# First sequence's 50-point transform with x as the stationary operand

## The chip, the cores and the metric

The kernel runs on one core of a Trainium2 chip. A core has a matrix engine (TensorE, PE in the profile; its weight loads are shown as PEld), a vector engine (DVE), a scalar engine (ACT), GpSimd (POOL) and a sync engine (SP), each with its own queue of instructions, and 16 DMA engines that serve all queues. Matmuls multiply a stationary operand, loaded first, with a moving one; their results go to PSUM, from where DVE or ACT fetch them. The metric is the device time of one execution in microseconds (us); lower is better.

## The reference

The input x has 8 sequences of 3200 positions with 256 channels. Each sequence is filtered in the frequency domain, and the result goes through a gated convolution:

```python
X = np.fft.rfft(x, axis=1)
Yr = Xr @ w_r - Xi @ w_i + b_r
Yi = Xr @ w_i + Xi @ w_r + b_i
Yr, Yi = soft threshold of each by 0.01
y = np.fft.irfft(Yr + 1j * Yi, n=3200, axis=1)
gate = sigmoid(causal depthwise convolution of y with conv_w, 5 taps)
out = (gate * (y @ w_val)) @ w_out
```

The weights `w_val`, `conv_w` and `w_out` come as float64 and are turned into float32 by integer operations on DVE. Channel matmuls split their operands into a high and a low part (three products each), transforms use plain f32.

## The kernel before

A transform of 3200 points is split as 50 x 64: position n = 64 n2 + n1. For each sequence b there are three stages, named in the code as follows.

- `p1(b, u, at)`, u from 0 to 7: the 50-point transform over n2. The table `f1` is stationary, x moves: positions n1 and 64 - n1 are taken together, in two halves of the partitions (50 rows at partition 0, 50 at partition 64). Each piece loads 4 + 4 positions (line 554, a helper that splits a load into 48 and 2 rows), makes its products into PSUM (lines 594, 599, 601), copies one half (ACT, line 607), adds and subtracts the two ("folds", DVE, line 613) and stores the result in DRAM as `a_dram` (lines 554 and 631). The store is there because the next stage needs another order of rows: the frequency and the position's half on the partitions.
- `p2(b, d, at)`, d from 0 to 6: loads rows of `a_dram` (line 650), makes the 64-point transform (`s2`, line 668, with `a` stationary and the table `f2` moving), splits the result into high and low parts, multiplies by the channel matrices (`mix_sum`, line 786, and `mix`, line 782), applies the threshold (lines 794, 796), transforms back over 64 points (`s1i`, line 737) and stores in DRAM as `z_dram` (line 753).
- `positions`, `conv`, `gated`: load `z_dram` (line 554), transform back over 50 points (`s2i`, line 848), convolve (lines 896, 899), project (lines 882, 878), and write the output (line 960).

Nothing is issued in the order of the Python loops. Every piece is given to a planner (`Plan`) with an engine, a cost, a due time made from the weights in the table `O`, and what it uses and sets. `Plan.order` simulates the engines: an engine takes among the pieces that are ready, within a slack, the one with the earliest due time, and that order is what each engine's queue holds. Buffers are slots of rotating pools (`SLOTS`); a piece that opens a buffer waits until the slot's former users are done. DMAs of nearly all kinds are issued from SP's queue. Where the planner sees PE idle between the times in `FILL`, it puts in matmuls of zeros (line 363), and at the start it puts matmuls of an idle buffer (`warm`, line 987).

For the first sequence `p1` has a form of its own (`early`): its loads are issued at once, the first on two queues, into buffers that later serve other ends (`x`, `zl`, `y_hl`). Four groups of warming lie between its pieces. The loads and casts of the channel matrices wait for some of these pieces (`BEHIND`, `START`), and later constants and the second sequence's loads of x wait for the first sequence's stores (`STORED`).

Of the kernel before, what the change touches and what calls it, by code (L numbers as in the profile page):

```python
# [10 lines left out]
F32 = mybir.dt.float32  # L11
# [21 lines left out]
def dft_constants():  # L33
# [67 lines left out]
    out = {"f1": f1.reshape(NH, N2, P), "f2": f2, "g1": g1, "g2": g2.reshape(Q, 2 * Q)}  # L101
# [169 lines left out]
CLOCK = ((28000, 1.6), (45000, 1.2))  # L271
FILL = 36000, 200000
# [9 lines left out]
def act(n, kind="copy"):  # L282
# [9 lines left out]
O = {'spread': -91.8948,  # L292
     'hold': 1.0724,
     'together': 1.2701,
     'later': -3.6572,
     'load_x': 9.9589,
     'p1': 0.1254,
     'p1_step': 1.2361,
     'load_a': -5.3199,
     's2': -1.7149,  # L300
     's1i': 1.553,
     'p3': 1.0966,
     'load_z': -28.9681,
     'y': 11.7985,
     'conv': 25.53,
     'val': 6.1049,
     'gate': -22.7084,
     'project': 7.8156,
     'late_val': 6.023,
     'late_out': 14.484,  # L310
     'turn': -55.8644,
     'pre': -4.984,
     'mix_sum': -1.4205,
     'p1_1': -7.3343,
     'load_x_1': -7.2435,
     'p1_2': -1.5627,
     'p3_0': 0.9988}
WARM = 2, 1, 1, 1, 8
# [8 lines left out]
def fourier_filter_then_gated_conv(ctx: ExitStack, tc: tile.TileContext, x, w_r, w_i, b_r, b_i,  # L327
                                   w_val, conv_w, w_out, f1, f2, g1, g2, out):
# [27 lines left out]
    y_sb = const.tile([P, 2, (N1 + KC - 1) * N2], F32, name="y_sb")  # L356
    mid_sb = const.tile([P, 2, 2, N2], F32, name="mid_sb")
# [47 lines left out]
    def sums(at):  # L405

        n = 2 * D
        for k, (name, sc, op) in enumerate((("w_n", -1.0, ALU.subtract), ("w_d", 1.0, ALU.subtract))):
            key = ("st", name)

            def make(k=k, key=key, sc=sc, op=op):
                r, i = (tl["st", m][:, 0:n] for m in (("w_r", "w_i") if k == 0 else ("w_i", "w_r")))
                out = room(key, "acc", 2 * D)
                tl[key] = out.rearrange("p (j d) -> p j d", j=2)
                nc.vector.scalar_tensor_tensor(out=out, in0=r, scalar=sc, in1=i, op0=ALU.mult, op1=op)
            add(at + 0.1 * k, "DVE", dve(n), make, [("st", "w_r", 0), ("st", "w_i", 0), *START], [key + (0,)], {key: "acc"})
# [75 lines left out]
    def load_bias(at):  # L492
# [23 lines left out]
        add(at, "PE", 2700, spread, [("b", 0, 0), ("b", 0, 1), ("turn", "p1", 7)], [k2 + (0,)], {k2: "ps_2"}, mode="f")  # L516
# [41 lines left out]
    START = [("turn", "start", h) for h in range(NH)]  # L558
# [5 lines left out]
    def p1(b, u, at):  # L564

        kx, kp, ks, ka = ("x", (b, u)), ("p1", (b, u)), ("s1", (b, u)), ("a_dram", b)
        early = b == 0
        x_tag = ("x" if u < 3 else "zl" if u < 6 else "y_hl") if early else "x"
        s_tag = ("s1", "g_hl", "xs")[u % 3] if early else "s1"
        p_tag = "ps_2"  # L570
        rows = ROWS

        def load(h):
            xt = room(kx, x_tag, 4 * D) if h in (0, None) else tl[kx]
            src = x[b].rearrange("(n m) c -> n (m c)", m=N1)
            for g in range(NH) if h is None else (h,):
                eng = QUEUES[g][1] if early and u < BOTH else nc.sync
                lo = (N1 - 3 - 4 * u if g else 4 * u) * D
                n = 3 * D if g and u == 0 else 4 * D
                by_rows(eng, xt[half(g), 0:n], src[:, lo:lo + n], rows)  # L580
                if n < 4 * D:
                    by_rows(eng, xt[half(g), n:], src[:, NM * D:(NM + 1) * D], rows)
        if early:
            for h in range(NH):
                add(-100 + u, QUEUES[h][0] if u < BOTH else "SP", 650, lambda h=h: load(h), (), [kx + (h,)], None if h else {kx: x_tag}, kb=200)
        else:
            add(at + O["load_x"] + O["load_x_1"] * (b == 1), "SP", 1300, lambda: load(None), STORED if b == 1 else (),
                [kx + (0,), kx + (1,)], {kx: x_tag}, kb=400, chain="x")

        def products():  # L590
            xt, p = tl[kx], two_banks(kp, p_tag)
# [42 lines left out]
        if early:  # L634
            STORED.append(("stored", 0, u))
        add(at + 0.02, "SP", 1500 + 1500 * (u == 0), store, [ks + (0,), ks + (1,)],
            [key] + ([STORED[-1]] if early else []), {ka: "a_dram"} if u == 0 else None, kb=400)


    def p2(b, d, at):  # L640
# [10 lines left out]
        add(at + O["load_a"], "SP", 700, load, A_KEYS[b], [ka + (0,)], {ka: "a"}, kb=128 * nt, chain="a")  # L651
# [3 lines left out]
        def s2(i):  # L655
            if i == 0:
                two_banks(k2, "ps_2")
            if last:
                for c in range(2):
                    nc.tensor.matmul(tl[k2][:, 0, c * P:(c + 1) * P], tl[ka][:, 0, c * P:(c + 1) * P], f2_sb[:, (NT - 1) * N1:], start=True, stop=True)  # L660
                return
            p = tl[k2].rearrange("p h (c t k) -> p h c t k", c=2, t=4)
            for t in (2 * i, 2 * i + 1):
                for c in range(2):
                    for h in range(NH):
                        for e in range(2):
                            rows = slice(h * HP, (h + 1) * HP)
                            nc.tensor.matmul(p[e * HP:(e + 1) * HP, h, c, t, :], tl[ka][rows, t, c * P + e * HP:c * P + (e + 1) * HP],  # L668
# [407 lines left out]
```

## Time and profile before

| | us |
|---|---|
| median of 3 runs (lowest, highest) | 858.8 (857.43, 858.82) |
| the profiled execution | 859.73 |
| its span, first to last instruction | 857.8 |
| PE busy in the span | 821.0 |
| DVE busy in the span | 736.2 |
| ACT busy in the span | 593.7 |

The mean granted TensorE clock is 0.973 of full speed; 162.27 MB were moved by DMA. The page divides the span into 40 slices of 21 us and gives, per slice, the busy tenths of each engine and the clock in tenths. A stretch view gives the same for chosen times. In the views, `L668` is line 668 of the kernel, `SPq` the sync engine's queue as it issues DMAs, `[0.79 <-DMA a<-a_dram]` an idle time of the engine in us and what ended it; `x58` counts instructions. An f32 matmul shows as two records of weight load and matmul.

### The profile page before, as it was taken

The numbers are of one execution on the slowest core, as the hardware profiler recorded it, in microseconds if no ns is written. First come the engines' busy times: TensorE is split into PE (matmuls) and PEld (weight loads), VectorE is DVE, ScalarE is ACT, GpSimd is POOL, SyncE is SP. The second block draws the span as 40 slices with busy tenths as digits, with TensorE's granted clock in tenths as the row PEclk, the third lists the DMA queues.
The fourth block names the chain that finished last, engine by engine and source line by source line (L and its number), as shares of the span: only waits on it lengthen the run. The fifth ranks groups of instructions, "written<-read, shape, count | busy, mean of one in ns | idle before, by whom it ended". The sixth has DMA issues, their size and how long they took to land.

```text
span 857.8 us, 23810 instructions
## 1 busy us (share of the span) xinstructions
PE 821.0 (96%) x9866; PEld 700.7 (82%) x9866; DVE 736.2 (86%) x1006; ACT 593.7 (69%) x903; POOL 4.5 (1%) x12
## 2 busy tenths in 40 slices
PE   8878867999999999999999999999999999999997
PEld 2456656889888988889988989899888999998874
DVE  3345679799998999899989998999989998998795
ACT  2234635778777786778777886878777787776753
POOL 0000000000000000000000000000001000000000
PEclk7888979999999999999999999999999999999999
DMA  6688889867886569776796759876895576225422
GB/s 169 182 190 224 246 214 250 228 179 191 209 234 185 165 180 258 203 204 174 224 245 195 192 175 248 206 206 187 231 234 158 157 200 193 71 83 173 133 76 96
DMA packets 125909, 162.27 MB, mean 189 GB/s; under 512 B 12528, under 2 KB 100234, under 8 KB 125802
## 3 DMA queue, kind: packets, MB, share of 16 engines
q1 hardware_dynamic: 125598, 160.34, 68.1%
q8 instruction: 78, 1.28, 0.7%
q10 hardware_dynamic: 204, 0.41, 0.2%
q14 instruction: 29, 0.24, 0.1%
HBM read 82.06 MB, written 78.64 MB: 187 GB/s over the span
## 4 chain that ended last, share of the span: by engine, by line
PE 69%; DVE 13%; DMA 9%; ACT 4%; SPq 3%; issue 2%; DVEq 0%; ACTq 0%
PE o_ps L882 13%; PE y_ps L782 12%; PE v_ps L882 11%; PE y_p L848 10%; PE y_ps L786 6%; DMA x<-in_x 4%; PE p L594 4%; PE s L668 4%; PE z_ps L737 4%; DVE acc L899 4%; PE v_ps L878 2%; SPq L554 2%; DMA zl<-z_dram 1%; DVE acc L933 1%; DVE gated L390 1%
## 5 line engine op out<-in xcount | busy, mean ns | idle before, releaser
L899 DVE SCALAR_TENSOR_TENSOR acc<-y_sb,cw_sb,acc 128x800 f32<-128x800 f32 x256 | 263.0, 1047 | 16.1 <-ACT acc L896 15.6
L782 PEld LDWEIGHTS y_ps<-w_sb,xs 128*128 128x128 f32 x1152 | 144.3, 191 | 28.4 <-DVE y_ps L788 12.4
L782 PE MATMUL y_ps<-w_sb,xs 128*128 128x256 f32 x1152 | 156.3, 286 | 11.1 <-DVE y_ps L788 11.0
L882 PE MATMUL o_ps<-gated,wo_sb 128*128 128x400 f32 x744 | 150.8, 349 | 0.8 <-DVE gated L390 0.8
L882 PEld LDWEIGHTS o_ps<-gated,wo_sb 128*128 128x128 f32 x744 | 134.6, 188 | 4.1 <-DVE gated L390 1.1
L882 PE MATMUL v_ps<-y_hl,wv_sb 128*128 128x400 f32 x648 | 128.4, 346 | 0.5 <-DVE s L613 0.5
L882 PEld LDWEIGHTS v_ps<-y_hl,wv_sb 128*128 128x128 f32 x648 | 115.4, 188 | 1.1 <-PE y_ps L786 0.7
L613 DVE TENSOR_TENSOR s<-p,s 128x512 f32<-128x512 f32 (+2 forms) x144 | 89.3, 626 | 27.5 <-ACT s L607 16.4
L848 PEld LDWEIGHTS y_p<-g_sb,zl 100*64 100x64 f32 x2048 | 89.1, 137 | 11.7 <-ACT y_ps L764 3.5
L848 PE MATMUL y_p<-g_sb,zl 100*64 100x100 f32 x2048 | 97.4, 251 | 0.7 <-DMA zl<-z_dram 0.5
L786 PE MATMUL y_ps<-w_sb,xs 128*128 128x256 f32 x576 | 90.0, 293 | 7.6 <-ACT y_ps L764 7.6
L786 PEld LDWEIGHTS y_ps<-w_sb,xs 128*128 128x128 f32 x576 | 79.3, 194 | 20.9 <-ACT y_ps L764 9.0
L794 ACT ACTIVATE tp<-y_ps,nlam 128x512 f32<-128x512 f32 (+1 forms) x104 | 70.0, 674 | 25.1 <-PE y_ps L782 25.1
L388 ACT CAST gated<-acc 128x800 fp32r<-128x800 f32 x62 | 53.3, 859 | 30.7 <-DVE acc L933 30.5
L601 PE MATMUL p<-x,f_sb 50*64 50x512 f32 x240 | 72.2, 654 | 1.7 <-DMA x<-in_x 1.7
L933 DVE TENSOR_TENSOR acc<-v_ps,acc 128x800 f32<-128x800 f32 x64 | 62.9, 984 | 11.4 <-PE v_ps L878 5.5
L796 DVE SCALAR_TENSOR_TENSOR tp<-y_ps,tp 128x512 f32<-128x512 f32 (+1 forms) x104 | 68.6, 661 | 4.1 <-ACT tp L794 4.0
L594 PE MATMUL p<-x,f_sb 50*64 50x512 f32 x256 | 71.6, 647 | 0.1
L668 PEld LDWEIGHTS s<-f_sb,a 64*64 64x64 f32 x3072 | 53.7, 137 | 19.5 <-issue 11.6
L909 ACT ACTIVATE acc<-acc 128x800 f32<-128x800 f32 x64 | 55.8, 878 | 16.3 <-DVE acc L899 16.0
L958 ACT COPY o<-o_ps 128x800 f32<-128x800 f32 x63 | 51.8, 822 | 21.3 <-PE o_ps L882 15.8
L716 DVE TENSOR_TENSOR sx<-s,sx 128x512 f32<-128x512 f32 x48 | 33.0, 688 | 38.2 <-ACT xs L713 37.2
(92 smaller groups left out, 1031.3 us busy)
## 6 DMA issues: line engine op xcount, KB each, us to landing
out<-o SPq DMA_DIRECT2D x126, 200.0 KB
a<-a_dram SPq DMA_DIRECT2D x96, 256.0 KB
z_dram<-z_t SPq DMA_DIRECT2D x48, 512.0 KB
zl<-z_dram SPq DMA_DIRECT2D x64, 384.0 KB
a_dram<-s SPq DMA_DIRECT2D x120, 192.0 KB
x<-in_x SPq DMA_DIRECT2D x119, 192.0 KB
a_dram<-s SPq DMA_DIRECT2D x120, 8.0 KB
x<-in_x SPq DMA_DIRECT2D x119, 8.0 KB
```

What stands on the lines that cost most here:

```text
L594: nc.tensor.matmul(p[k * HP:(k + 1) * HP, 0, :], f1_sb[half(0), 0:HP], xt[half(0), k * 512:(k + 1) * 512], start=True, stop=True)
L601: nc.tensor.matmul(dst, f1_sb[half(1), 0:HP], back[:, 2 * k:2 * k + 2, :], start=True, stop=True)
L613: nc.vector.tensor_tensor(out=st()[lo:hi, h, n], in0=tl[kp][lo:hi, 0, n], in1=st()[lo:hi, 1, n], op=(ALU.add, ALU.subtract)[h])
L668: nc.tensor.matmul(p[e * HP:(e + 1) * HP, h, c, t, :], tl[ka][rows, t, c * P + e * HP:c * P + (e + 1) * HP], f2_sb[rows, (4 * d + t) * N1: ...
L782: nc.tensor.matmul(p[:, 1 - r, :], xm(hx, c, r, i), w_sb[:, m, hw, c, :], start=False, stop=k == 5, skip_group_check=True)
L786: nc.tensor.matmul(tl[ky][:, 0], sm(hx, c, i), w_sb[:, 0, hw, c, :], start=False, stop=k == 5, skip_group_check=True)
L794: nc.scalar.activation(out=buffer(kt, "tp", [P, 2, D])[:, 0:n], in_=tl[ky][:, 0:n], func=AF.Relu, bias=nlam)
L796: add(at + 0.2, "DVE", dve(n * D), lambda: nc.vector.scalar_tensor_tensor(out=tl[kt][:, 0:n], in0=tl[ky][:, 0:n], scalar=LAM, in1=tl[kt][: ...
L848: nc.tensor.matmul(dst[e * HP:(e + 1) * HP], zt[0:Q, m, c * P + e * HP:c * P + (e + 1) * HP], g, start=True, stop=True)
L882: nc.tensor.matmul(p[:, e, 0:TB], w[:, hw, c, e * P:(e + 1) * P], src(hy, c), start=n == 0, stop=n == 5)
L899: nc.vector.scalar_tensor_tensor(out=acc(c), in0=wide(c, j), scalar=cw_sb[:, c, j:j + 1], in1=acc(c), op0=ALU.mult, op1=ALU.add)
L933: add(at + O["gate"], "DVE", dve(2 * TB), lambda: nc.vector.tensor_tensor(out=part(), in0=by_half(tl[kv][:, :, 0:TB]), in1=part(), op=ALU. ...
```

## The change

The first sequence has a stage of its own, `p0`, and `p1` serves the other seven. In `p0` x is the stationary operand, and a new table `f0`, a folded form of `f1` with 100 rows, moves. x is loaded as `x0_sb` with the two halves one after the other on 100 partitions and in two parts of 128 channels. For each channel, four matmuls take its 32 positions of each half (100 rows by 32 columns, one position of 128 channels after the other) against 25 columns of `f0` each and write 32 partitions each. So the rows come out in the order that `s2` needs, and the sum over the 100 rows does the folding. Groups of 32 channels share a PSUM buffer; DVE adds each group into `a0_sb`, from which `s2` of the first sequence reads directly. Position 0 and the middle position, which have no partner, go through two matmuls, a copy and four small DMAs between SBUF and SBUF into the rows of `a0_sb` beforehand; the addition leaves them as they are. No `a_dram` is written or read for the first sequence.

`x0_sb` and `a0_sb` take memory that other buffers use later: `a0_sb` lies in `y_sb`, and `x0_sb` in a new tile `big`, in which the slots of `acc`, `zl` and `a` are now slices, rotated by hand. Warming is 4 + 4 matmuls at the start rather than 2, 1, 1, 1 and 8 between the pieces. The waits `START`, `BEHIND` and the first `STORED` are empty. The planner's clock model and the time from which it fills in zeros begin earlier, and its weights `O` have new values.

```diff
-CLOCK = ((28000, 1.6), (45000, 1.2))
-FILL = 36000, 200000
+CLOCK = ((10000, 1.6),)
+FILL = 9000, 200000
...
-O = {'spread': -91.8948,
...
+O = {'spread': -119.1399,
...
-WARM = 2, 1, 1, 1, 8
+WARM = 4, 4
...
+    a0_sb = y_sb.rearrange("p c n -> p (c n)")[:, 0:NT * D].rearrange("p (t c) -> p t c", c=D)
+
+    big = const.tile([P, 2 * 4 * TB + 5 * MB * D], F32, name="big")
+    x0_sb = big[:, 0:NM * D].rearrange("p (g m c) -> p g m c", g=2, m=NM)
+    f0_sb = const.tile([P, NH * N2], F32, name="f0_sb")
...
-    START = [("turn", "start", h) for h in range(NH)]
+    START = []
...
+    def p0(at):
+
+        k0, kp, ks = ("x", (0, 0)), ("p1", (0, 0)), ("s1", (0, 0))
+        src = x[0].rearrange("(n m) c -> n m c", m=N1)
+
+        def begin():
+            xt = room(k0, "x", 4 * D)
+            for h in range(NH):
+                nc.scalar.dma_start(out=xt[half(h), 0:D], in_=src[:, h * NM])
+            for h in range(NH):
+                nc.scalar.dma_start(out=f1_sb[h * HP:h * HP + N2, :], in_=f1[h])
+            nc.scalar.dma_start(out=f0_sb[0:Q, :], in_=f0)
+        add(-300, "ACT", 1800, begin, (), [("f0", 0, 0), ("f1", 0, 0), k0 + (0,)], {k0: "x"}, kb=240)
...
+        add(-200, "POOL", 600, lambda: nc.gpsimd.memset(x0_sb[0:Q, :, 0], 0.0), (), [("x0_sb", 0, 0)] + [k + (0,) for k in keys],
+            {k: k[0][3:] for k in keys})
+        for g in range(2):
+            def load(g=g):
+                for h in range(NH):
+                    c = slice(g * P, (g + 1) * P)
+                    rows_ = src[:, N1 - 1:NM:-1, c] if h else src[:, 1:NM, c]
+                    by_rows(nc.sync, x0_sb[h * N2:(h + 1) * N2, g, 1:], rows_, ROWS)
+            add(-190 + g, "SP", 1300, load, (), [parts[g]], kb=1800)
+
+        add(-200, "DVE", 3500, lambda: nc.vector.memset(a0_sb, 0.0), (), [("a0", 0, j) for j in range(8)])
+
+        def first():
+            xt, p = tl[k0], two_banks(kp)
+            for h in range(NH):
+                nc.tensor.matmul(p[0:HP, h, 0:D], f1_sb[half(h), h * HP:(h + 1) * HP], xt[half(h), 0:D], start=True, stop=True)
...
+        def spread():
+            st = tl[ks].rearrange("p (h n) -> p h n", h=NH)
+            for g in range(NH):
+                for r in range(2):
+                    q = g * HP + r * NM
+                    nc.scalar.dma_start(out=a0_sb[q:q + 1], in_=st[r:N2:2, 1 - g if r else g, 0:D])
...
+        for j in range(8):
+            kj = ("p0", j)
+
+            def products(j=j, kj=kj):
+                p = two_banks(kj)
+                for i in range(32):
+                    out = p[:, i // 16, (i % 16) * NT:(i % 16 + 1) * NT]
+                    w = x0_sb[0:Q, j // 4, :, j % 4 * 32 + i]
+                    for q in range(4):
+                        nc.tensor.matmul(out[q * NM:(q + 1) * NM], w, f0_sb[0:Q, q * NT:(q + 1) * NT], start=True, stop=True)
...
+            def evict(j=j, kj=kj):
+                dst = a0_sb[:, :, j * 32:(j + 1) * 32].rearrange("p t (b c) -> p b t c", b=2)
+                src_ = tl[kj][:, :, 0:16 * NT].rearrange("p b (c t) -> p b t c", t=NT)
+                nc.vector.tensor_tensor(out=dst, in0=src_, in1=dst, op=ALU.add)
+            add(-50 + 4 * j, "DVE", dve(800), evict, [kj + (0,)], [("a0", 0, j)])
...
-        add(at + O["load_a"], "SP", 700, load, A_KEYS[b], [ka + (0,)], {ka: "a"}, kb=128 * nt, chain="a")
+        if b:
+            add(at + O["load_a"], "SP", 700, load, A_KEYS[b], [ka + (0,)], {ka: "a"}, kb=128 * nt, chain="a")
+        a_keys = [ka + (0,)] if b else [("a0", 0, j) for j in range(8)]
+        a_of = lambda: tl[ka] if b else a0_sb[:, 4 * d:4 * d + nt]
...
+    for v in range(len(WARM)):
+        add(-100 + v, "PE", WARM[v] * 860, lambda v=v: warm(v, WARM[v]),
+            [ki + (0,)], [kw + (0,), kv + (0,), ("seeds", 0, 0)], None if v else {kw: "ps_y", kv: "ps_y"}, chain="warm")
+    p0(0)
+    BEHIND = []
+    load_bias(-59)
```

More of the change, by code (lines that the diff above doesn't have):

```diff
@@ L291 @@
 T = float(NU)
-O = {'spread': -91.8948,
[L293 to L308, printed above, removed]
+O = {'spread': -119.1399,
+     'hold': -0.215,
+     'together': 1.6937,
+     'later': 90.8159,
+     'load_x': 26.1614,
+     'p1': 1.2136,
+     'p1_step': 1.1385,
+     'load_a': 24.5799,
+     's2': -1.2947,
+     's1i': 1.0277,
+     'p3': 4.3919,
+     'load_z': -21.5415,
+     'y': 27.3596,
+     'conv': 29.9494,
+     'val': 4.7604,
+     'gate': 28.9402,
+     'project': 7.0607,
      'late_val': 6.023,
      'late_out': 14.484,
[L311 to L317, printed above, removed]
-WARM = 2, 1, 1, 1, 8
+     'turn': -49.0259,
+     'pre': -30.5631,
+     'mix_sum': -52.8515,
+     'p1_1': -3.3115,
+     'load_x_1': 26.2803,
+     'p1_2': -0.3998,
+     'p3_0': 0.1142}
+WARM = 4, 4
 SLOTS = {"x": 3, "zl": 3, "y_hl": 2, "s1": 2, "a": 2, "xs": 2, "sx": 1, "xz": 1, "tp": 3, "zst": 2,
@@ L566, in p1, with load @@
         kx, kp, ks, ka = ("x", (b, u)), ("p1", (b, u)), ("s1", (b, u)), ("a_dram", b)
[L567 to L570, printed above, removed]
         rows = ROWS
[L573 to L574 removed]
+        def load():
+            xt = room(kx, "x", 4 * D)
             src = x[b].rearrange("(n m) c -> n (m c)", m=N1)
[L576 to L577 removed]
+            for g in range(NH):
                 lo = (N1 - 3 - 4 * u if g else 4 * u) * D
                 n = 3 * D if g and u == 0 else 4 * D
[L580 removed]
+                by_rows(nc.sync, xt[half(g), 0:n], src[:, lo:lo + n], rows)
                 if n < 4 * D:
[L582 to L588, printed above, removed]
+                    by_rows(nc.sync, xt[half(g), n:], src[:, NM * D:(NM + 1) * D], rows)
+        add(at + O["load_x"] + O["load_x_1"] * (b == 1), "SP", 1300, load, (), [kx + (0,), kx + (1,)], {kx: "x"}, kb=400, chain="x")
         def products():
[L591 removed]
+            xt, p = tl[kx], two_banks(kp)
             back = xt.rearrange("p (m c) -> p m c", c=D)[half(1), ::-1, :]
@@ L970, in late_weights @@
         add(at, "POOL", 3000, make, [A_KEYS[B - 1][-1], *[("w", n, h) for n in ("w_val", "w_out") for h in ("high", "low")]], [key + (0,)], {key: "x"})
-    def begin():
-        for h in range(NH):
-            nc.sync.dma_start(out=f1_sb[h * HP:h * HP + N2, :], in_=f1[h])
-    add(-200, "SP", 800, begin, (), [("f1", 0, 0)], kb=40)
     ki, kw, kv = ("idle", 0), ("warm", 0), ("warm", 1)
@@ L989, in fourier_filter_then_gated_conv @@
     add(-199.5, "POOL", 200, lambda: nc.gpsimd.memset(zero_sb, 0.0), (), [("zero", 0, 0)])
-    add(-199, "POOL", 300, lambda: nc.gpsimd.memset(y_sb[:, :, 0:H0 * N2], 0.0), (), [("y", "back", 0)])
-    for v in range(5):
-        add(-42 + 4 * v, "PE", WARM[v] * 860, lambda v=v: warm(v, WARM[v]),
-            [ki + (0,), *([("turn", "p1", 2 * v - 1)] if v else [])], [kw + (0,), kv + (0,), ("seeds", 0, 0)], None if v else {kw: "ps_y", kv: "ps_y"})
-        if v < 4:
-            for u in (2 * v, 2 * v + 1):
-                p1(0, u, -40 + 2 * u)
-    BEHIND = [("turn", "p1", 3)]
-    load_bias(-31)
+    for v in range(len(WARM)):
[4 more added lines that the diff above has]
+    load_bias(-59)
     load_matrix(-90, "w_r", w_r, w_sb[:, 0], BEHIND)
@@ L1034, in fourier_filter_then_gated_conv @@
                 later_constants(u)
+        if b == 0:
+            add(T + O["p3"] - 12, "POOL", 300, lambda: nc.gpsimd.memset(y_sb[:, :, 0:H0 * N2], 0.0), (), [*[("a0", 0, j) for j in range(8)], ("y", "back", 0)])
         start = (b + 1) * T + O["p3"] + O.get(f"p3_{b}", 0.0)
```

55 lines of the change are left out of this document (38 added, 17 removed).

## The prediction

> **What bounds the kernel now.** I read the page first, then the stretches of time, the chain of waits of the first 48 us, the instructions in order of time there, and the waits from 40 to 150 us.
>
> ```profile
> span 857.8 us, 23810 instructions
> ...
> PE 821.0 (96%) x9866; PEld 700.7 (82%) x9866; DVE 736.2 (86%) x1006; ACT 593.7 (69%) x903; POOL 4.5 (1%) x12
> ...
> PE   8878867999999999999999999999999999999997
> ...
> PEclk7888979999999999999999999999999999999999
> DMA  6688889867886569776796759876895576225422
> ```
>
> ```profile
> 0.00:20.00 20.00, 16.59 (x50) 4.80 (x50) 6.71 (x12) 4.66 (x8) 1.29 (x10) 0.72 0.69 171
> 20.00:46.00 26.00, 21.04 (x90) 10.71 (x88) 9.19 (x15) 5.72 (x11) 0.00 (x0) 0.83 0.69 186
> 46.00:150.00 104.00, 83.30 (x1121) 63.74 (x1121) 71.62 (x133) 51.30 (x87) 0.00 (x0) 0.88 0.86 224
> 150.00:250.00 100.00, 98.39 (x1454) 87.14 (x1455) 91.60 (x126) 80.10 (x126) 0.00 (x0) 1.00 0.78 209
> 350.00:450.00 100.00, 100.00 (x1271) 89.38 (x1271) 94.66 (x128) 76.97 (x118) 0.00 (x0) 1.00 0.76 209
> ```
>
> A row of the second view is start:end, length, busy time (and instructions) of PE, weight loads, DVE, ACT and POOL, granted TensorE clock, DMA share, GB/s. From 150 us on PE is full at clock 1.00: whatever the opening saves moves the end by as much, and nothing later can absorb it, unless the new order of work makes PE wait there. Before 150 us PE isn't full, and its clock is down to 0.72 to 0.88. So the case is decided in the first 150 us.
>
> ```profile
> 1.44 3.73 DMA x<-in_x
> ...
> 17.02 3.17 DMA x<-in_x
> 20.27 0.79 SPq L631
> ...
> 37.56 3.37 DMA a_dram<-s
> ...
> 40.99 0.68 SPq L650
> ```
>
> ```profile
> 1.56 16.09 SPq L554 DMA_DIRECT2D x<-in_x  x28
> ...
> 18.64 1.53 SPq L554 DMA_DIRECT2D a_dram<-s  x4
> ...
> 20.27 2.86 SPq L631 DMA_DIRECT2D a_dram<-s  x4
> ...
> 23.23 1.49 SPq L554 DMA_DIRECT2D a_dram<-s  x4
> ...
> 26.42 11.80 SPq L554 DMA_DIRECT2D a_dram<-s  x24
> ```
>
> ```profile
> 46.03 1.87 PE L668 MATMUL s<-f_sb,a 64*64 64x64 f32 x58 [0.79 <-DMA a<-a_dram]
> ...
> 54.04 0.97 PE L786 MATMUL y_ps<-w_sb,xs 128*128 128x256 f32 x6
> ...
> 55.82 1.15 PEld L668 LDWEIGHTS s<-f_sb,a 64*64 64x64 f32 x64 [0.53 <-issue]
> ```
>
> The chain of the opening is DMA and the SP queue almost throughout: x comes in until 20 us, SP issues the stores of `a` until 38 us, the last store lands at 41 us, `a` comes back, and the 64-point stage (L668) runs at 46.03. In that time PE does 8 small pieces of the transform; the rest is warming and zeros. The change cuts into this chain.
>
> **The change part by part.**
>
> *Loads.* x arrives as 8 DMAs instead of 34: 100 rows by 31 positions by 256 channels by 4 bytes, 3.17 MB in two halves by channel. The code's runs are 128 channels, 512 bytes; no row of before shows a large transfer of that run length, so I bound it.
>
> ```profile
> q1 hardware_dynamic: 125598, 160.34, 68.1%
> q8 instruction: 78, 1.28, 0.7%
> ```
>
> The mean packet of q1 has 1277 bytes and takes 0.681 x 16 x 857.8 us / 125598 = 74 ns of one engine. 3.17 MB are 6200 packets of 512 bytes, 388 for each of 16 engines: 11.5 us if a packet costs by bytes (30 ns), 28.8 us if each costs the full 74 ns. In between lies the rate of the first 20 us above, 171 GB/s, when x was nearly the only traffic: 18.6 us. I take that, since it has the same source and start. From 1.6 us the halves land at 10.9 and 20.2 us; the ends for the second are 13 and 30.
>
> *Warming* falls from 13 matmuls to 8 (two records each).
>
> ```profile
> L987 PE MATMUL warm<-idle 128*128 128x512 f32 x26 | 17.9, 835 | 1.5 <-DVE idle L978 1.5
> L613 DVE TENSOR_TENSOR s<-p,s 128x512 f32<-128x512 f32 (+2 forms) x18 | 11.4, 632 | 16.2 <-ACT s L607 8.6 <-ACT s L609 7.3
> L607 ACT COPY s<-p 128x512 f32<-128x512 f32 x8 | 4.7, 585 | 20.4 <-PE p L601 11.8 <-DMA x<-in_x 5.6 <-DMA a_dram<-s 3.0
> L978 DVE MEMSET idle<- 128x512 f32 x1 | 0.5, 485 | 0.9 <-PEq L1061 0.9
> ```
>
> 16 records at 17.9/26 us take 11 us, so PE is free at about 12 us, just after the first half has landed.
>
> *The products.* 32 matmuls in pieces of 512 columns go, and 1024 come: 100 rows by 32 columns of x stationary, 25 columns of `f0` moving, four column tiles side by side. By the rows every f32 matmul of this kernel is two records (s2 has 32 matmuls and 64 records), so 2048 pairs of weight load and matmul. None of this shape is in the trace. The nearest is s2: 64 pairs issued in 1.15 us, 18.0 ns a pair, with 64 weight columns and 64 moving ones, also on four tiles. Upper end: 18.0 ns whatever the size, 36.9 us in all. Lower end: by the 32 weight columns, half, 9.0 ns (18.4 us). The fetch of instructions sets almost the same floor: q8 moves blocks of 16 KB, 0.007 x 16 x 857.8/78 = 1.23 us each; 1.28 MB over 2 x 9866 PE instructions is about 64 bytes each, so a block holds 128 pairs, 9.6 ns a pair. I take 9.6: columns, not the issue, look to set s2's price, since its weights and its moving columns both shrink by half or more. A stage of 128 matmuls is then 2.46 us, all eight 19.7 us. Stride is a further unknown: the stationary columns lie 512 bytes apart, which no weight load of before does; it is inside the same two ends.
>
> The trace speaks here against a rule of the Trainium skill, "TensorE: Matmul & The Clock Gate", section "Wait — 56ns, not 53.3ns?": matmuls never start closer than about 25 ns, however few columns they have. s2's 18.0 ns on four tiles is below that already, so it isn't a floor over all tiles; if it held for this shape, 2048 pairs would be an estimated 51 us, the slower rival below.
>
> The first four pieces run from 12 to 21.8 us. The second half has landed at 20.2, so the other four run to 31.6. If it lands at 30 they end at 40.
>
> *Folding.* Eight additions on DVE from PSUM take the place of 18 folds.
>
> ```profile
> L933 DVE TENSOR_TENSOR acc<-v_ps,acc 128x800 f32<-128x800 f32 x64 | 62.9, 984 | 11.4 <-PE v_ps L878 5.5 <-PE v_ps L882 3.9 <-ACT acc L909 1.9
> ```
>
> The nearest has the same 800 elements: 0.98 us, less at L613's rate (0.63 us for about 512, so 0.98 again), at most double if PSUM's stride of 25 costs. Seven lie beside the products; the last lies on the path, with about 0.2 us of semaphores. So s2 can begin at 31.6 + 1.2 = **32.8 us instead of 46.03**, 13.2 us earlier. DVE and ACT lose 11.4 and 4.7 us of work that lay beside other things: worth nothing. The zeroing of `a0` is 6400 elements, 12.5 times the 0.485 us memset, 6.1 us on a DVE idle until 13: hidden by the wait for x. POOL's two memsets are hidden likewise.
>
> *Position 0* goes its own way: a load of x, two matmuls, a copy, four DMAs of single rows, all on ACT's queue. L631's four, their equals, took SP 2.86 us. They wait for the two matmuls behind the warming, so issue at about 13 to 16 us and land by 19; the first addition waits for that, and three PSUM buffers let PE go on for three pieces (to 19.4), so it is just hidden. Behind it on ACT are the weight casts, whose data come no earlier than 24 us. Each s2 of the first sequence now waits for all eight additions, and nothing else but constants: 14 loads of `a` are gone.
>
> *Queues.* SP loses 17.7 us of store issues (the four rows with `a_dram<-s`), the loads and 6.55 MB of traffic (100 x 32 x 1024 bytes out and back). The loads of the second sequence, at 42.43 us before, can follow the weights at about 24 us.
>
> *After s2.*
>
> ```profile
> PE y_ps L782 <- DVE y_ps L788: 11.0, 3, 7.6
> ...
> PE y_ps L786 <- ACT y_ps L764: 6.6, 3, 4.5
> ...
> PE s L668 <- DMA a<-a_dram: 5.0, 2, 4.2
> ...
> PE s L668 <- DMA f_sb<-in_f: 2.5, 1, 2.5
> ...
> PEld p L601 <- DMA x<-in_x: 1.2, 2, 0.8
> ```
>
> Waits of 40 to 150 us: total, times, longest. DMA ended only 0.8 (5.0 less the 4.2 ahead of 46.03) + 2.5 + 1.2 = 4.5 us of PE's idle after 46 us; with 6.55 MB less ahead of these transfers I let them go. The largest, 7.6 us, is DVE turning float64 weights into float32 in one run:
>
> ```profile
> 108.92 2.15 DVE L430 TENSOR_SCALAR st<-st 128x512 int32<-128x512 int32 x5
> ...
> 115.73 0.62 ACT L388 CAST wv_sb<-st 128x512 fp32r<-128x512 f32 x1 [6.88 <-DVE st L436]
> ```
>
> That work stays, and I credit nothing for it.
>
> Sum, against the profiled execution's own 859.7 us (its span is 857.8): 859.7 - 13.2 - 4.5 = 842.0. It lies 0.9 above the median shown, so **841 us**.
>
> **The rivals.**
>
> *Much faster.* The DMA's relief reaches further than the waits named. By 150 us before moved 20 x 171 + 26 x 186 + 104 x 224 kB = 31.6 MB; without 6.55 it is 25.0. At 224 GB/s after the first 20 us (3.4 MB), the same state is reached at 20 + 21.6/0.224 = 116 us. PE's 83.3 us of work from 32.8 on ends at 116 as well. 34 us earlier: 825. For it: DMA share 0.86 in this stretch, PE clock 0.88. Against: the longest waits there are on DVE and ACT.
>
> *No change: s2's price.* Pairs at 18.0 ns: products 12 to 48.9 us, s2 at 50.1, 4.1 later; less 4.5: 858.
>
> *Slower: the narrow pairs cost more than s2's.* Place: PE's products, on which everything waits. The 58 pairs of s2 at 46.03 took 32.2 ns each, in a stretch of low clock; halfway between that and 18.0 is 25 ns, 51.4 us in all. s2 begins at 12 + 51.4 + 1.2 = 64.6, 18.6 later; less 4.5, less 0.9: 873. It decides from 12 + 2048 p + 1.2 - 46.03 = 4.5, p = 18.2 ns. (The floor of 25 ns in the Trainium skill's clock-gate page, above, would give the same time by another mechanism.) For it: PE may wait for x between warming and products and lose its clock (0.72 here), and block fetches may not overlap. Against: half the columns, dense issue, and zeros that the plan now adds from 9 us. "Runtime: NRT & Kernel Launch", section "Instruction fetch mechanics", of the Trainium skill says that PE holds 2048 instructions and that the fetch is mostly hidden; no row here shows a burst that long.
>
> *Given back later.* The planner's weights all change, and `acc`, `zl` and `a` become slices of one tile. If PE waits 3% more in the 600 us from 150 to 750, 18 us go: 859. Against: slot counts and engines' work there are unchanged.
>
> **How the numbers follow.** Forecast 0.50 (own range 832 to 850: second half from 13 to 30 us and pairs of 9 to 13 ns), much faster 0.18, s2's price 0.11, slower 0.12, given back 0.09. A measurement of this kernel can tell about 0.2%, 1.7 us. Faster: the first two and, from partial forms of the others that leave over 1.7 us, 0.08, so 0.76; same 0.08; slower 0.16 (0.12 and 0.04 of giving back). The range is 822 to 862: it takes in both price bounds and leaves out the slower rival and the far edge of the much faster one.
>
> **What would show it.** x's second half landed and the last product done near 32 us, s2 (L668's successor) near 33; 128 matmuls in 2.3 to 2.6 us; no `a_dram` traffic before the second sequence's; PE full from about 132 us. Products at 18 ns a pair, additions of 2 us, a granted clock of 0.5 between 12 and 30 us, or PE under 98% after 150 us would make it wrong.

## The result, and the profile after

The changed kernel takes 894.78 us (median of 4 runs, 891.31 to 896.37) against 858.12 us (855.35 to 858.82, 4 runs) for the kernel before on the same chip: a ratio of 1.0428, 95% interval 1.0386 to 1.047. It is 36.7 us **slower**. The forecast was 841 us and its range ended at 862, so the prediction is wrong, and on the wrong side. The profiled execution took 893.55 us.

The page of the changed kernel (the line numbers are its own: L700 are the products, L707 the additions, L741 the 64-point stage, L955 the projections):

```profile
span 891.7 us, 27633 instructions
...
PE 860.9 (97%) x11818; PEld 751.3 (84%) x11818; DVE 765.4 (86%) x997; ACT 615.8 (69%) x895; POOL 4.3 (0%) x13
...
PE   7999997899999999999999999999999999999997
...
PEclk9955998999999999999999999999999999999999
DMA  9401777886779658965697758965794566227322
...
q8 instruction: 93, 1.52, 0.7%
```

PE has 2 x (11818 - 9866) = 3904 instructions more than before, and PE and DVE look busier. The DMA row says more: its second to fourth slices (22 to 89 us) read 4, 0 and 1, where the kernel before had 6, 8 and 8. From the third slice on the memory traffic has all but stopped, so this is no longer the opening in which the transfers set the pace.

The stretches of time, columns as before (start:end, length, busy time and instructions of PE, weight loads, DVE, ACT and POOL, clock, DMA share, GB/s):

```profile
0.00:20.00 20.00, 14.50 (x95) 7.80 (x96) 5.88 (x2) 2.05 (x3) 1.17 (x10) 0.91 1.00 151
20.00:46.00 26.00, 25.30 (x726) 24.18 (x723) 8.86 (x7) 9.22 (x2) 0.00 (x0) 0.93 0.42 104
46.00:150.00 104.00, 96.14 (x2140) 82.27 (x2139) 77.71 (x105) 57.26 (x69) 0.44 (x1) 0.77 0.47 131
150.00:250.00 100.00, 95.42 (x1438) 81.42 (x1437) 89.44 (x132) 76.18 (x122) 0.00 (x0) 0.98 0.76 209
350.00:450.00 100.00, 98.42 (x1240) 87.53 (x1240) 92.60 (x125) 75.71 (x117) 0.00 (x0) 1.00 0.72 203
...
50.00:60.00 10.00, 10.00 (x351) 10.00 (x350) 7.62 (x2) 10.00 (x4) 0.00 (x0) 0.50 0.02 5
20.00:30.00 10.00, 9.83 (x342) 9.66 (x340) 0.00 (x0) 0.27 (x1) 0.00 (x0) 1.00 0.63 153
```

The last two rows carry the case. Between 20 and 30 us PE does 342 pairs of weight load and matmul at clock 1.00, between 50 and 60 us 351 at clock 0.50: 29 and 28.5 ns each, whatever the clock. In the second stretch the only thing that moves is 5 GB/s.

The chain of waits up to 120 us (start, length, what), and the instructions in order of time there:

```profile
1.72 8.90 DMA f_sb<-in_f
10.76 1.03 PE p L676 x4
11.79 5.17 PE warm L1056 x8
16.96 1.34 PE p L373 x12
18.30 5.42 PE p L700 x143
...
41.74 3.25 PE bias L530 x8
44.99 1.71 PE bias L532 x4
46.69 36.49 PE p L700 x926
...
86.74 0.98 PE s L741 x64
```

```profile
18.23 20.83 PE L700 MATMUL p<-f_sb,big 100*32 100x25 f32 x701
...
26.66 3.02 ACTq L688 DMA_DIRECT2D y_sb<-s  x4
27.50 60.81 SPq L571 DMA_DIRECT2D x<-in_x  x22
29.73 9.22 ACT L405 CAST w_sb<-st 128x512 fp32r<-128x512 f32 x2 [17.32 <-DMA y_sb<-s]
34.29 5.47 DVE L707 TENSOR_TENSOR y_sb<-p,y_sb 128x800 f32<-128x800 f32 x2 [26.22 <-DMA y_sb<-s]
...
83.22 0.99 DVE L707 TENSOR_TENSOR y_sb<-p,y_sb 128x800 f32<-128x800 f32 x1 [3.81 <-PE p L700]
```

Where x and SP's queue held the opening of the kernel before, the products now hold it alone: from 18.2 to 83.2 us the chain is PE, 60 us of products and 5 us of bias between them. The last addition ends at 84.2, and the 64-point stage starts at 86.6 us instead of 46.0 (the first 4 of its 64 records there ran at 44.8). SP sits in the second sequence's loads of x for 60.8 us: their slots wait for `p1` of that sequence, which stands behind the products on PE, so the transfers stop as well. And two small things look odd: a weight cast takes 4.6 us (0.62 before) and an addition 2.7 us (forecast 0.98).

### The profile page after: what moved, and what is told of

Its sections match the earlier page's. It is cut to its first block, busy times and chain, and to the rows that moved or that the text cites. A ratio compares the mean times of both kernels' runs of the same rounds, so it can differ in the third digit from the quotient of the medians.

```text
span 891.7 us, 27633 instructions
## 1 busy us (share of the span) xinstructions
PE 860.9 (97%) x11818; PEld 751.3 (84%) x11818; DVE 765.4 (86%) x997; ACT 615.8 (69%) x895; POOL 4.3 (0%) x13
## 4 chain that ended last, share of the span: by engine, by line
PE 65%; DVE 13%; ACT 11%; DMA 8%; issue 2%; SPq 1%; ACTq 0%; DVEq 0%
PE o_ps L955 12%; PE v_ps L955 11%; PE y_ps L855 8%; PE y_p L921 7%; PE p L700 7%; PE y_ps L859 5%; DMA big<-z_dram 3%; PE s L741 3%; PE z_ps L810 3%; ACT xs L786 3%; DVE big L972 2%; DVE s L620 2%; PE v_ps L951 2%; DMA a_dram<-s 2%; PE p L601 2%
## 5 line engine op out<-in xcount | busy, mean ns | idle before, releaser
L972 DVE SCALAR_TENSOR_TENSOR big<-y_sb,cw_sb,big 128x800 f32<-128x800 f32 x256 | 261.2, 1044 | 11.1 <-ACT big L969 8.9
L955 PE MATMUL o_ps<-gated,wo_sb 128*128 128x400 f32 x744 | 154.7, 352 | 3.6 <-ACT xs L793 3.0
L955 PEld LDWEIGHTS o_ps<-gated,wo_sb 128*128 128x128 f32 x744 | 132.9, 188 | 8.5 <-ACT xs L793 3.7
L955 PE MATMUL v_ps<-y_hl,wv_sb 128*128 128x400 f32 x648 | 129.7, 347 | 3.3 <-DVE xs L790 1.3
L955 PEld LDWEIGHTS v_ps<-y_hl,wv_sb 128*128 128x128 f32 x648 | 115.4, 188 | 5.6 <-ACT xs L793 3.6
L921 PEld LDWEIGHTS y_p<-g_sb,big 100*64 100x64 f32 x2048 | 89.4, 137 | 16.4 <-issue 6.5
L921 PE MATMUL y_p<-g_sb,big 100*64 100x100 f32 x2048 | 99.9, 252 | 0.2
L969 ACT ACTIVATE big<-y_sb,cw_sb 128x800 f32<-128x800 f32 x64 | 60.8, 964 | 15.6 <-DVE gated L407 15.5
L405 ACT CAST gated<-big 128x800 fp32r<-128x800 f32 x62 | 53.3, 859 | 25.2 <-DVE big L1006 24.6
L1006 DVE TENSOR_TENSOR big<-v_ps,big 128x800 f32<-128x800 f32 x64 | 62.7, 981 | 7.7 <-PE v_ps L955 5.7
L982 ACT ACTIVATE big<-big 128x800 f32<-128x800 f32 x64 | 55.4, 876 | 14.5 <-DVE big L972 14.2
L405 ACT CAST y_hl<-y_sb 128x800 fp32r<-128x800 f32 x54 | 46.3, 857 | 24.0 <-PE v_ps L955 23.8
L407 DVE TENSOR_TENSOR gated<-big,gated 128x800 fp32r<-128x800 f32 x62 | 60.8, 981 | 1.4 <-ACT gated L405 0.9
L700 PEld LDWEIGHTS p<-f_sb,big 100*32 100x32 f32 x2048 | 58.9, 236 | 1.7 <-issue 1.6
```

Of the source, the lines that this page charges most:

```text
L405: nc.scalar.copy(out=high(), in_=src())
L407: add(at + 0.001, "DVE", dve(n), lambda: nc.vector.tensor_tensor(out=low(), in0=src(), in1=f32(high()), op=ALU.subtract), [*uses, hl[0]], ...
L700: nc.tensor.matmul(out[q * NM:(q + 1) * NM], w, f0_sb[0:Q, q * NT:(q + 1) * NT], start=True, stop=True)
L921: nc.tensor.matmul(dst[e * HP:(e + 1) * HP], zt[0:Q, m, c * P + e * HP:c * P + (e + 1) * HP], g, start=True, stop=True)
L955: nc.tensor.matmul(p[:, e, 0:TB], w[:, hw, c, e * P:(e + 1) * P], src(hy, c), start=n == 0, stop=n == 5)
L972: nc.vector.scalar_tensor_tensor(out=acc(c), in0=wide(c, j), scalar=cw_sb[:, c, j:j + 1], in1=acc(c), op0=ALU.mult, op1=ALU.add)
```

## The experiments

**What a pair costs, and why.** Two causes fit 28.5 ns: the stride of the stationary operand (its columns lie 512 bytes apart), or the sheer count of instructions. The first run takes the stride away and keeps the count.

```diff
-                    w = x0_sb[0:Q, j // 4, :, j % 4 * 32 + i]
+                    n = (j % 4 * 32 + i) * 32
+                    w = x0_sb[0:Q, j // 4].rearrange("p m c -> p (m c)")[:, n:n + 32]
```

> The 32 stationary columns of each product are 32 neighbouring words instead of 32 words 512 bytes apart; every load, matmul, addition and the planned order stay (so the first sequence's transform is made of the wrong channels and its output is meaningless). Theory 'stride': the pair of weight load and matmul costs 28.5 ns because the weight load reads words 512 bytes apart; it falls to 9 to 16 ns, 128 matmuls to 2.3 to 4.1 us, and DVE and ACT run at their usual durations meanwhile (a cast of 128x512 0.62 us instead of 4.6 to 6). s2 then begins at 45 to 58 us instead of 86.6, the time is 855 to 872. Theory 'count': the cost is per instruction (issue or the fetch of instructions); pairs stay at 28 to 29 ns, the time at 891 to 898.

891.98 us (one execution). Its PE in order of time, and its stretches (of PE and weight loads of this line alone, then clock, DMA share and GB/s):

```profile
18.25 1.83 PE L701 MATMUL p<-f_sb,big 100*32 100x25 f32 x189
23.50 1.30 PE L701 MATMUL p<-f_sb,big 100*32 100x25 f32 x128 [3.42 <-issue]
...
31.78 1.92 PE L701 MATMUL p<-f_sb,big 100*32 100x25 f32 x128 [2.36 <-issue]
35.51 1.92 PE L701 MATMUL p<-f_sb,big 100*32 100x25 f32 x128 [1.81 <-issue]
...
49.97 1.95 PE L701 MATMUL p<-f_sb,big 100*32 100x25 f32 x127 [1.09 <-issue]
...
79.66 1.28 PE L701 MATMUL p<-f_sb,big 100*32 100x25 f32 x81 [1.54 <-issue]
```

```profile
31.70:33.80 2.10, 1.92 (x128) 1.80 (x128) 0.50 0.45 114
60.00:70.00 10.00, 5.09 (x350) 4.85 (x353) 0.50 0.02 5
```

The products have become fast and the kernel has not. The first 189 run in 1.83 us, 9.7 ns a pair, close to the price that the prediction took. Then they come in bursts of 128 (now and then 127), at 10 ns (15 ns at clock 0.50), and between the bursts PE stands still for 1.1 to 3.4 us with nothing to wait for but its own next instruction. The pauses don't fall on the ends of the pieces, 256 pairs, where the PSUM buffer changes. 128 pairs are 256 instructions, and 256 times 64 bytes is one 16 KB block of q8. From 60 to 70 us 350 pairs are done with PE half idle, and the 5 GB/s are the blocks: 350 x 128 bytes in 10 us are 4.5 GB/s. From 49.97 to 79.66 us nine bursts start, 3.71 us apart in the mean. So the instructions arrive at one block per 3.7 us, 29 ns a pair, while DMA share is 0.02 and next to nothing competes with them. In the changed kernel the packets of q8 show the same: through the products a block starts every 3.3 to 4.7 us (but once, over the bias matmuls) and takes 0.9 to 1.4 us; the rest of each interval is empty, as if each block were asked for only when an earlier one is used up. In the contiguous run, from 49.97 us on, a block's packet starts 1.0 to 1.2 us after a burst has begun.

Padding the channels from 128 to 130 floats makes the stride 520 bytes and leaves the result whole.

```diff
-    x0_sb = big[:, 0:NM * D].rearrange("p (g m c) -> p g m c", g=2, m=NM)
+    x0_sb = big[:, 0:2 * NM * 130].rearrange("p (g m c) -> p g m c", g=2, m=NM)
...
-                    by_rows(nc.sync, x0_sb[h * N2:(h + 1) * N2, g, 1:], rows_, ROWS)
+                    by_rows(nc.sync, x0_sb[h * N2:(h + 1) * N2, g, 1:, 0:P], rows_, ROWS)
```

> The pitch of x in the on-chip memory is 130 words (520 bytes) instead of 128; nothing else changes, the result stays exact. If the stride is slow because 512 bytes always meets the same bank, pairs fall to 9 to 16 ns as with neighbouring words and the time to 855 to 872. If any stride beyond a line is slow, or the cost is per instruction, pairs stay at 28 to 29 ns and the time at 891 to 898.

891.95 us, 1.0394 (1.0372 to 1.0416) of the kernel before.

```profile
24.64 2.29 PE L700 MATMUL p<-f_sb,big 100*32 100x25 f32 x128 [2.52 <-issue]
...
31.43 1.14 ACT L405 CAST w_sb<-st 128x512 fp32r<-128x512 f32 x2 [18.33 <-DMA f_sb<-in_f]
33.19 2.28 PE L700 MATMUL p<-f_sb,big 100*32 100x25 f32 x128 [1.69 <-issue]
```

A pair now takes 17.8 ns in the bursts, at clock 1.00 and at 0.50 alike, the pauses are shorter by what the bursts are longer, and the end hardly moves. A cast is back at 0.57 us. So the stride of 512 bytes is a second wall of the same height, not the one that can be taken away with profit: in the changed kernel the first 180 pairs, whose instructions were there beforehand, took 5.00 us, 27.8 ns each at clock 1.00, just under the 29 ns of the supply, which is why its products show next to no pauses. The third run goes the other way and gives PE four times the columns (contiguous again, all 100 columns of `f0` in each matmul).

```diff
-                        nc.tensor.matmul(out[q * NM:(q + 1) * NM], w, f0_sb[0:Q, q * NT:(q + 1) * NT], start=True, stop=True)
+                        nc.tensor.matmul(out[q * NM:(q + 1) * NM], w, f0_sb[0:Q, 0:Q], start=True, stop=True)
```

> As e1_contig, but each product moves all 100 columns of f0 instead of 25 (the values are meaningless again): the same 2048 pairs, four times the moving columns. With neighbouring stationary words the pairs came in bursts of 128 in 1.2 to 1.9 us, with 2 to 3.4 us of nothing between, as many instructions as one 16 KB block holds. Theory 'supply' (blocks of instructions arrive one per 3.65 us): the pauses take up the extra columns; bursts of 128 grow to about 2.8 us (22 ns a pair at 88 ns per 100 columns on four tiles), and the products still end near 81 us, the time stays at 888 to 896. Theory 'PE': pauses of 2.3 us stay between bursts, and the products take 15 to 25 us longer, the time 905 to 917.

894.23 us (one execution).

```profile
33.02 2.95 PE L701 MATMUL p<-f_sb,big 100*32 100x100 f32 x128 [1.33 <-issue]
...
62.37 2.95 PE L701 MATMUL p<-f_sb,big 100*32 100x100 f32 x128 [0.40 <-issue]
```

23 ns a pair rather than 10 to 15, and it costs next to nothing: the pauses shrink. Bursts of 1.92, 2.29 and 2.95 us all fit into the same interval, the packets of the blocks start as soon after a burst's beginning as before (1.0 to 1.2 us from 55.6 us on), and the last addition ends at 82.0, 84.2 and 84.0 us in the three runs (84.2 in the changed kernel). The supply of instructions sets the time.

**Is the rest of the idea worth what was forecast?** Every fourth product alone, still 100 columns wide, makes 512 pairs: 4 blocks instead of 16.

```diff
-                for i in range(32):
+                for i in range(0, 32, 4):
...
-                        nc.tensor.matmul(out[q * NM:(q + 1) * NM], w, f0_sb[0:Q, q * NT:(q + 1) * NT], start=True, stop=True)
+                        nc.tensor.matmul(out[q * NM:(q + 1) * NM], w, f0_sb[0:Q, 0:Q], start=True, stop=True)
```

> As e6_wide100, but only every fourth product is made, 100 columns wide, so that it fills the room of four (the other channels are left out, the output is meaningless): 512 pairs, 4 blocks of instructions. Theory 'supply': the products fall from some 62 us to 10 to 17 us, s2 begins at 36 to 44 us instead of 86.6. This is the opening that the prediction had in mind. If the rest follows as forecast from there but for the cost of the new planner's weights (2.9 us for each of five or six sequences): 850 to 862. If the opening's end doesn't carry through, 870 or more.

860.42 us, 1.0042 (1.0023 to 1.006). The same with the kernel before's weights `O`:

> e10_quarter with the planner's old weights. If these cost nothing in the steady part (95.4 us a sequence as before): 835 to 850, which would be the prediction's 841 had the products been cheap. If the changed kernel's other buffers or order cost it anyway: 852 to 862.

858.36 us, 1.0009 (0.9993 to 1.0025): 34 and 38 us below the runs with all products, but no gain on the kernel before, so my expectation of 835 to 850 missed. PE of the run with the new weights, and DVE of the one with the old:

```profile
20.24 4.40 PE L701 MATMUL p<-f_sb,big 100*32 100x100 f32 x192
34.24 3.75 PE L530 MATMUL bias<-b_sb 1*128 1x256 f32 x8 [9.60 <-DVE y_sb L708]
37.78 1.91 PE L532 MATMUL bias<-b_sb 1*128 1x256 f32 x4
39.62 9.22 PE L701 MATMUL p<-f_sb,big 100*32 100x100 f32 x320
```

```profile
25.80 5.69 ACTq L688 DMA_DIRECT2D y_sb<-s  x4
...
34.29 2.79 DVE L708 TENSOR_TENSOR y_sb<-p,y_sb 128x800 f32<-128x800 f32 x3 [26.22 <-DMA x<-in_x]
```

With products at 14 us in all, position 0 comes to light: its four row transfers are issued at 25.8 us, not at 13 to 16, the first addition starts at 34.3, PE runs out of PSUM buffers after three pieces, and the bias matmuls behind it are late as well. Two more runs leave out these four transfers (one line), with the old weights and the new:

```diff
-        add(-60, "ACT", 1300, spread, [ks + (0,)], [("a0", 0, j) for j in range(8)], kb=100)
```

> As the run with a quarter of the products and the old weights (858.36 us), and also without the four row transfers of position 0, so that no addition waits for them: position 0 and three channels of four are left out of the first sequence. Theory 'with cheap products the change is held up by position 0 and by x, and an earlier 64-point stage does move the end': the additions start right behind the first products (19 to 21 us rather than 34.3), the pause of the products from 24 to 41 us shrinks to the wait for x's second half and the bias (about 27 to 33), the 64-point stage begins near 42 rather than 54.9, and the time is 845 to 852 us. Rival 'what the opening saves is absorbed later': the stage begins near 42 all the same and the time stays at 856 to 861.

> The same with the change's own weights; position 0 and three channels of four are left out of the first sequence. If the new weights cost a fixed sum per sequence, whatever the opening does, this is 2 to 12 us above the run with the old weights (the pair with position 0 differed by 860.42 - 858.36 = 2.1, the kernel before by 15): 850 to 862 us. If their cost depends on the opening, the difference is under 1 us.

850.87 us (0.9922, 0.9894 to 0.995) and 852.71 us (0.9939, 0.9916 to 0.9963). In the first:

```profile
18.08 4.31 PE L700 MATMUL p<-f_sb,big 100*32 100x100 f32 x189
19.73 0.99 DVE L707 TENSOR_TENSOR y_sb<-p,y_sb 128x800 f32<-128x800 f32 x1 [11.66 <-PE p L700]
...
32.25 10.24 PE L700 MATMUL p<-f_sb,big 100*32 100x100 f32 x320
...
42.56 0.99 DVE L707 TENSOR_TENSOR y_sb<-p,y_sb 128x800 f32<-128x800 f32 x1 [0.38 <-PE p L700]
```

The last addition ends at 43.55 rather than 51.42, 7.9 us earlier, and the time is 7.5 us lower. What the opening saves does reach the end.

All runs with the new stage together, each with the end of its last addition and the span of the same profiled execution:

| run | last addition ends | span | span less it |
|---|---|---|---|
| quarter, no position 0, new weights | 42.75 | 850.5 | 807.8 |
| quarter, no position 0, old weights | 43.55 | 850.4 | 806.9 |
| quarter, new weights | 49.91 | 856.5 | 806.6 |
| quarter, old weights | 51.42 | 857.8 | 806.4 |
| contiguous | 82.00 | 890.2 | 808.2 |
| contiguous, 100 columns | 84.00 | 892.4 | 808.4 |
| stride 520 bytes | 84.21 | 891.0 | 806.8 |
| the change | 84.21 | 891.7 | 807.5 |
| the change with the old weights | 84.80 | 889.7 | 804.9 |
| interleaved (below) | 89.74 | 902.8 | 813.1 |

But for the last, 805 to 808 us follow the last addition, whether it ends at 43 or at 85 us.

**The weights.** The new weights in the kernel before, and the old ones in the changed kernel:

> The kernel before with the planner's new weights O alone. From the first y_p to the end the changed kernel takes 720.0 us instead of 705.0, with PE at 98.4% instead of 99.6% from 150 to 750 us. Theory 'order': the new weights cost this; here PE falls to about 98.4% and the time rises to 865 to 875. Theory 'mismatch': the loss comes from an opening that ran 50 us later than planned; here the steady part stays at 99.6% and the time within 6 us of before.

> The changed kernel with the planner's old weights O. Theory 'order': 8 to 15 us of the loss go, 880 to 887. Theory 'mismatch': the steady part stays at 98.4%, and the time at 890 to 900.

```diff
-O = {'spread': -91.8948,
...
+O = {'spread': -119.1399,
```

The kernel before with the new weights: 873.18 us, 1.0181 (1.0153 to 1.0208). The changed kernel with the old: 895.94 us, 1.0448 (1.042 to 1.0475). One sequence in the middle, from its first transform back over 50 points to the next sequence's, in the kernel before and then in the changed one, as stretches:

```profile
425.10:520.50 95.40, 95.40 (x1229) 85.78 (x1228) 90.05 (x122) 74.14 (x114) 0.00 (x0) 1.00 0.74 208
```

```profile
438.10:536.50 98.40, 96.75 (x1229) 85.91 (x1228) 90.92 (x122) 74.05 (x113) 0.00 (x0) 1.00 0.73 200
```

The same 1229 matmuls take 98.4 us rather than 95.4, with 1.65 us of PE idle; the kernel before with the new weights has 98.2 us too. That looks like something given back later, and in the kernel before the new weights cost 15 us. With the new opening they make 2 us or less, either way: 894.78 against 895.94, 860.42 against 858.36, 852.71 against 850.87 us. The new weights bring the third sequence's `y` forward there (298.8 against 316.1 us in the pair without position 0) and lose it again by the end.

The stretch is not the weights' alone. In the quarter run with the old ones the sequence in the same place takes 98.0 us too, with PE full:

```profile
421.80:519.80 98.00, 98.00 (x1241) 87.42 (x1240) 92.47 (x125) 76.15 (x116) 0.00 (x0) 1.00 0.74 205
```

What differs is how long PE stands idle (a stretch's length less PE's busy time), from the start of its first 64-point stage to the first transform back over 50 points (`y_p`), and from there to the end:

| run | stage starts | first `y_p` | idle between | idle after | PE busy, both |
|---|---|---|---|---|---|
| before, old weights | 46.0 | 152.8 | 20.7 | 7.7 | 783.4 |
| before, new weights | 46.5 | 157.1 | 20.1 | 13.1 | 794.6 |
| the change, old weights | 88.3 | 174.3 | 12.0 | 8.9 | 780.5 |
| the change, new weights | 86.6 | 171.7 | 11.6 | 13.0 | 780.5 |
| quarter, old weights | 54.9 | 142.7 | 13.6 | 8.6 | 780.7 |
| quarter, new weights | 50.5 | 136.2 | 12.8 | 13.7 | 779.5 |
| no position 0, old weights | 47.0 | 135.1 | 12.6 | 8.6 | 782.1 |
| no position 0, new weights | 43.4 | 130.8 | 13.2 | 13.2 | 780.8 |

In every pair the new weights cost 4 to 5 us of idle time behind the first `y_p`; with the new stage, part of that comes back because the 64-point stage starts 2 to 4 us sooner. In the kernel before they cost 11 us of busy time besides, which they don't in the others, and why is open.

**Hiding the supply.** If PE waits for blocks, the second sequence's `p1`, with few and long instructions, could run in between. For this the stride was 520 bytes, the weights the old ones, the planner's cost of a piece 7300 ns, and its due times such that it alternated the two.

```diff
-            add(-50 + 4 * j, "PE", 2300, products, [parts[j // 4], ("x0_sb", 0, 0), ("f0", 0, 0), *[k + (0,) for k in keys[(0, 2)[j // 4]:(3, 7)[j // 4]]]],
+            add(-9 + 1.24 * j, "PE", 7300, products, [parts[j // 4], ("x0_sb", 0, 0), ("f0", 0, 0), *[k + (0,) for k in keys[(0, 2)[j // 4]:(3, 7)[j // 4]]]],
...
-            add(-50 + 4 * j, "DVE", dve(800), evict, [kj + (0,)], [("a0", 0, j)])
+            add(-9 + 1.24 * j, "DVE", dve(800), evict, [kj + (0,)], [("a0", 0, j)])
```

> The whole computation, exact: pitch of 130 words, the planner's old weights, the products priced at 7.3 us for each of the eight groups (two blocks of instructions), and the second sequence's p1 pieces put between the groups. By 'supply' the p1 pieces cost few instructions and run in the pauses, so their 9 us of PE and their stores are got for nothing: s2 at 78 to 86 us, the first y_p at 150 to 165 (171.7 changed, 152.8 before), the time 858 to 880. If PE's time sets the products, the pieces come on top: s2 at 90 us or later, and no gain over 890.

904.61 us, 1.0544 (1.0517 to 1.0571): worse. The 64-point stage starts at 92.0 us, so it is the branch that I had named for PE's own time, not that of the supply.

```profile
64.49 2.51 PE L700 MATMUL p<-f_sb,big 100*32 100x25 f32 x136
68.97 2.19 PE L700 MATMUL p<-f_sb,big 100*32 100x25 f32 x120 [1.98 <-issue]
71.09 1.12 PE L601 MATMUL p<-x,f_sb 50*64 50x512 f32 x2
```

Each piece of 256 pairs still contains pauses of 0.7 to 2.2 us, and `p1`'s matmuls, some 2.5 us a turn (71.09 to 73.64), cover less than a block's interval. So the blocks still held the products, and the pieces of `p1` came on top: in five of their seven turns between the products no block's packet starts, as if blocks were asked for only while PE uses up the products' many instructions. The pieces ended 5.5 us later than in the changed kernel, and 5.6 us more were lost behind them, which I did not follow up.

## Why the prediction was wrong, by its own steps

**The step that failed is the products' price.** 9.6 ns a pair, 19.7 us in all, was forecast; 2048 pairs took 60 us, 29.3 ns each in the mean. The term was mis-sized by a factor of 3, and by a mistake of method: I worked out how long one block of instructions is under way (1.23 us, about right: 0.9 to 1.4) and took that as the supply's rate, 128 pairs each 1.23 us. That assumes that the next block is under way when one lands. The trace of before showed durations of blocks, but no burst that used them up, so nothing in it said how often they can follow one another. It is one in 3.7 us. The upper bound, s2's 18.0 ns, failed for the same reason: s2 runs 64 pairs at a time, half a block.

Its lower bound was right for what it described: contiguous pairs with their instructions at hand took 9.7 ns. The stride, put "inside the same two ends", was outside them too (27.8 ns), and either alone would have made the change slower by the prediction's own break-even of 18.2 ns.

The error goes through the sum like this. Forecast: the last product at 31.6, its addition done about 1 us later at 32.6, and a span of 840.1 (842.0 less the 1.9 that before's profiled execution had outside its span), so 807.5 us behind it. Measured: 84.2, and 807.5 us. The 51.6 us between are the later start (18.2 rather than 12: 6.2), the bias matmuls, which I had not put in PE's way (4.9), and the products (60.0 rather than 19.6: 40.4).

**Loads, warming.** The first products started at 18.2 us, not 12. The two matmuls of position 0 stand ahead of the second half of the warming, and their table landed only at 10.6 (1.72 + 8.90), behind x's own transfers; so eight records of warming and the zeros ran from 11.8 to 18.3. The rate was near the forecast's at first, 151 GB/s against 171 over 20 us, but x's last packet landed at 26.6 us rather than 20.2 (97% had by 22), inside the bounds of 13 and 30. Of the changed kernel's work it held up position 0 alone.

**Position 0.** "Just hidden" was wrong by more than 10 us: issue at 26.66 rather than 13 to 16, just as x had come in. In the changed kernel the slow products hide it; with cheap ones it costs 7.5 us (858.36 to 850.87). The trace names what ACT's four transfers waited for: the entry ahead of them in ACT's queue waits for semaphores 101 and 105. DVE's zeroing was the last to set 101 before it, at 8.09 us. Semaphore 105 is the one that x's seventh load, issued at 15.04, sets and that the first of the four transfers uses as well; it was last set at 26.56, and the entry went through at 26.58. In the quarter runs the same two times are 25.07 and 25.09, and 25.70 and 25.72. So a semaphore shared with a load of x held position 0; one of its own was not tried.

**Folding.** The last addition and the third took 0.99 us as forecast. The other six, beside strided weight loads, took 2.7 to 2.9 us in the mean, and no product waited for them.

**After s2.** The 4.5 us credited there, and "nothing given back", gave 807.5 us behind the last addition, and 807.5 were measured. That they agree so well is luck: errors cancel. By the table of idle time, PE idled 9.1 us less than in the kernel before between the 64-point stage and the first `y_p`, not 4.5, and 5.3 us more after it, not nothing; its busy time fell by 2.9, and the stage began 2.4 us after the last addition rather than 0.2 (9.1 - 5.3 + 2.9 - 2.2 = 4.5). So the rival of giving back came true with 5 of its 18 us, and with the old weights with 1. The waits on DMA that the credit named are gone, but 0.8 of the 4.5 was counted twice: the wait for `a` of 0.79 us ended at 46.03 itself and so was inside the 13.2 already.

**The rivals.** The slower one had the place and the sign: PE's products, "block fetches may not overlap", decided from p = 18.2 ns. Its price, 25 ns, gave 873; of the 21.8 us that it still lacked, the products take 8.6 (60.0 rather than 51.4), the start 6.2 and the bias 4.9. I gave it 0.12. The rule of the Trainium skill that I weighed for it, in "Runtime: NRT & Kernel Launch", section "Instruction fetch mechanics", says that crossing a block is mostly hidden; this case's trace disagrees for instructions of 5 to 12 ns, with pauses of 0.4 to 3.4 us after bursts of 128 pairs. The floor of about 25 ns in the Trainium skill's "TensorE: Matmul & The Clock Gate", section "Wait — 56ns, not 53.3ns?", would have come near the time by another way; 9.7 ns a pair in bursts shows that it is not what held here.

**The marks** named for a wrong prediction mostly showed: products above 18 ns, additions above 2 us, PE under 98% after 150 us (95.42 of 100 in the first stretch). The granted clock did not (1.00 from 20 to 30 us), and a pair took as long at 0.50 later.

**What would be left.** With 4 blocks instead of 16 and position 0 left out (so with a result that is not whole), the kernel gains 0.8% (0.5 to 1.1) on the one before. Of its 43.6 us up to the last addition, 10 lie between two groups of products, where PE waits for the bias's input, which lands behind x, and multiplies the bias. No version tried here that computes everything beats it.

## What to carry to other kernels

Count instructions before nanoseconds: a stage that replaces a few long matmuls by thousands of short ones can be paced by the blocks in which instructions arrive (here 256 per 3.7 us, 14.5 ns for each), and then neither a better layout nor, as here, more or less work per instruction moves its end. A price taken from a burst shorter than a block says nothing about a longer one, and the time that one transfer takes is not the interval at which transfers come. Where a stage ends a known time before the end of the kernel, a table of that end against the span, as above, shows whether an opening or what follows it has failed; a second mark further on shows whether an agreement is a sum of errors that cancel.

## What the runs showed of the hardware

- PE's instructions came in blocks of 16 KB, one per 3.7 us, with DMA share at 0.02; one block took 0.9 to 1.4 us. Where the pairs took 10 to 23 ns, PE stood still after 128 of them (0.4 to 3.4 us).
- Pairs of a 100x32 weight load and a matmul with 25 columns, on four column tiles: 9.7 ns with contiguous stationary columns at clock 1.00, 15 ns at 0.50; 17.8 ns at a stride of 520 bytes at either clock; 27.8 ns at 512 bytes at clock 1.00.
- While PE loaded weights at a stride of 512 bytes, ACT and DVE slowed down: in the mean a 128x512 cast took 4.6 to 6.1 us (0.62 in the kernel before), an addition of 128x800 2.7 to 2.9 (0.99). At 520 bytes and with contiguous columns both had their usual times (0.57 and at most 0.99).
